# An attention kernel whose opening is written in another order, with the shifts of its first pairs set anew

## The chip, the core and the metric

The kernel runs on one core of a Trainium2 chip. Five engines work beside each other and meet only at semaphores: TensorE (PE, with its weight loads as PEld), VectorE (DVE), ScalarE (ACT), GpSimd (POOL) and SyncE (SP), which here only issues DMAs; ACT issues a few as well. The metric is the device time of one execution in microseconds (us); lower is better.

## The reference

Attention with a causal mask and a bias made of running sums, then two MLPs over all tokens, all in fp32:

```python
def _attn_ref(q, k, v, s):                      # (4, 8, 576, 64), s (4, 8, 576)
    scores = scale * np.matmul(q, k.transpose(0, 1, 3, 2))
    cum = np.cumsum(np.maximum(s, 0.0), axis=-1)
    bias = -(cum[:, :, :, None] - cum[:, :, None, :])
    scores = np.where(causal, -1000000000.0, scores + np.minimum(bias, 0.0))
    scores = scores - np.max(scores, axis=-1, keepdims=True)
    attn = np.exp(scores)
    attn = attn / (np.sum(attn, axis=-1, keepdims=True) + 1e-09)
    return np.matmul(attn, v)

def _moe_ref(x, w_in, w_out, alpha):            # 2304 tokens, 512 -> 2048 -> 512
    h = x @ w_in
    return (np.maximum(h, 0.0) + alpha * np.minimum(h, 0.0)) @ w_out
# the second MLP has r * r, r = max(h, 0), in the middle
```

## The kernel before

Two heads form a pair; there are 16 pairs, numbered 0 to 15. For accuracy each fp32 operand is split into a rounded part (`hi`) and a rest (`lo`), and the matmuls run on the parts. For one pair the work is: load q and k (`load_qk`, a main piece of 256 KB and a tail of 32 KB each), split them (`hi` is one pass, `lo` a subtraction; tiles `hl_q`, `hl_k`), turn them on TensorE (`pp`, L348, and `pp_tail`, L373, into the banks `ps_tr`), copy the turned parts out of the banks into `QS`, `QM`, `KS`, `KH`, and then for five row blocks i and two heads h: scores (`qk`, L419 with `KS`,`QS` and L420 with `KH`,`QM`; L425 for the last block), the row minimum on DVE (`red`, L446), the exponential on ACT (`exp`, L459), the transposes of the result (`tr`, L527), and the two products with v (`pv_a` L561, `pv_b` L577). Rows 64 and 65 of `KH` hold the two parts of the running sum of the pair's heads and meet two rows of ones in `QM`; so L420 of a pair needs those rows. For pair 0 they come straight from the tile `cum_hl` (named pt), for every later pair by a DMA from the DRAM tensor `cumD` (`cum_rows`, L397, two rows of 2304 bytes for each head).

Three things set the order. The opening, L691 to L771, is written out by hand: clearing, loads, splits, transposes and copies of pair 0, the splits of pair 1, and the loads of v for both. After it a list, `PIPE`, gives each step of a pair a place in a period and an offset in periods; a table `RAMP` adds to that place a shift for one step of one pair, and the steps are sorted by the sum. A table `WARM` puts matmuls on zeros, called fillers here (`keep_warm`, L700, out `ps_xa`, in `iv`), behind steps of pair 0. `in_order()` ties the instructions of each engine, and the DMA issues of SP, into that order. Pairs 4 and up go by `PIPE` and the few entries of `RAMP` that the change leaves alone. The MLPs follow, from about 195 us on.

Buffers that matter below: q and k of pairs n and n + 2 share `raw_q0`/`raw_k0` or `raw_q1`/`raw_k1` (so `raw_q0` is pair 0, then 2, then 4), scores have three banks, turned parts four.

Of the kernel before, what the change touches and what calls it, by code (L numbers as in the profile page):

```python
# [8 lines left out]
F32 = mybir.dt.float32  # L9
# [10 lines left out]
def attention_then_two_mlps(  # L20
# [13 lines left out]
    nc = tc.nc  # L34
# [654 lines left out]
        chain["at"] = len(traced)  # L689

    zero = apool.tile([P, S], F32, name="iv", tag="iv", bufs=1)  # L691
    nc.vector.memset(zero, 0.0)
    zero = zero.bitcast(F32R)
    blank = [None]

    def keep_warm(k, cols=512):
        if blank[0] is None:
            blank[0] = ps_x.tile([P, 512], F32, name="ps_xa", tag="ps_x")
        for _ in range(k):
            nc.tensor.matmul(blank[0][:, :cols], zero[:, 0:P], zero[:, :cols], start=True, stop=True)  # L700

    nc.scalar.dma_start(s_sb, s.rearrange("b h c -> (b h) c"))
    load_qk(0, 0)
    load_qk(0, 1, nc.scalar)
    warm = apool.tile([1, 1], F32, name="warm", bufs=1)
    nc.vector.memset(warm, 0.0)
    nc.scalar.activation(warm, warm, AF.Exp)
    keep_warm(10)
    init_persistent(0)
    nc.vector.memset(cum, 0.0)  # L710
    nc.vector.tensor_scalar(s_sb, s_sb, 0.0, None, ALU.max)
    nc.vector.tensor_tensor_scan(cum, s_sb, cum, 0.0, ALU.add, ALU.add)
    for x in range(2):
        load_qk(1, x)

    def kview(a, c):
        return a.rearrange(c, t=4)

    def bank_of(x, h):
        return kview(banks["pp", x, h].bitcast(F32), "p (t c) -> p c t")  # L720

    def qs_out(n, h):
        nc.scalar.activation(kview(QS[n][:, h, P:], "p (c t) -> p c t"), bank_of(0, h), AF.Copy, scale=SCALE)

    def qm_out(h):
        nc.vector.tensor_scalar(kview(QM[0][0:64, h, P:], "p (c t) -> p c t"), bank_of(0, h)[0:64], SCALE, None, ALU.mult)

    def kh_out(n, h, part):
        if part == 1:
            nc.scalar.copy(kview(KH[0][0:64, h, 0 : 4 * P], "p (c t) -> p c t"), bank_of(1, h)[64:128])  # L730
# [5 lines left out]
    hi(0, 0, 0, H1)
    hi(0, 1, 2, H0)
    lo(0, 1, 2, H0)
    hi(0, 1, 2, H1)
# [12 lines left out]
    nc.sync.dma_start(cumD, cum_hl.bitcast(F32))
    load_v(0)
    kh_out(0, 0, 0)
    qm_out(0)
    kh_out(0, 0, 1)
    kh_out(0, 1, 2)
    qs_out(0, 1)
    kh_out(0, 1, 1)
    qm_out(1)  # L760
    pp_tail(0)
    keep_warm(2)
# [814 lines left out]
```

## Time and profile before

| | us |
|---|---|
| median of 3 runs (lowest 950.13, highest 954.41) | 950.86 |
| the profiled execution, as timed | 952.03 |
| its span on the chip | 950.2 |
| PE busy | 936.9 (99%) |
| DVE busy | 770.4 (81%) |
| ACT busy | 607.1 (64%) |
| POOL busy | 280.3 (29%) |

The span runs from the first to the last recorded instruction; 1.83 us of the timed execution lie around it. Matmuls are pipelined and their ends are modelled, so two that follow each other overlap in the records; the distance of two starts tells what one costs. An idle time is given with the engine that ended it, found from the last semaphore that came; where that engine had long been done, it was another, often a DMA.

### The profile page before, as it was taken

The page shows a single profiled execution, that of the slowest core. Times are in us where ns is not written, and L with a number is a line of the kernel's source. Part 1 is how long each engine was busy: PE and PEld are TensorE (multiplying, and loading weights), DVE is VectorE, ACT ScalarE, POOL GpSimd, SP SyncE. Part 2 cuts the span into 40 slices and gives each one's busy share as a digit, 9 for nine tenths or more (in the row PEclk, how much of TensorE's full clock was granted, in tenths as well). Part 3 has the DMA queues.
Part 4 walks back from the last instruction along what each step waited for, and adds up shares of the span by engine and source line. Part 5 has one row for each costly group of instructions (what it writes and reads, how often), then busy time and mean ns, then how long its engine had stood idle before and what let it go on. Part 6 is the DMA issues. An engine that isn't in the chain of part 4 may idle for free.

```text
span 950.2 us, 16991 instructions
## 1 busy us (share of the span) xinstructions
PE 936.9 (99%) x5909; PEld 882.6 (93%) x5909; DVE 770.4 (81%) x1446; ACT 607.1 (64%) x1272; POOL 280.3 (29%) x278
## 2 busy tenths in 40 slices
PE   7999999999999999999999999999999999999998
PEld 6888888899999899999999999999999999999998
DVE  7788878868778987789778878788988888888685
ACT  6999988856566565577666656566445664456432
POOL 7466555134233212322102100344003530045200
PEclk9999999999999999999999999999999999999999
DMA  5787765337666758989568562586755867448384
GB/s 148 197 210 205 198 156 139 87 103 252 208 198 228 275 192 301 341 276 311 168 214 261 184 200 82 163 314 217 244 182 164 273 222 261 146 118 287 118 259 134
DMA packets 141063, 195.69 MB, mean 206 GB/s; under 512 B 50962, under 2 KB 102674, under 8 KB 135602
## 3 DMA queue, kind: packets, MB, share of 16 engines
q1 hardware_dynamic: 140384, 194.11, 65.1%
q8 instruction: 47, 0.77, 0.3%
q10 hardware_dynamic: 594, 0.50, 0.2%
q14 instruction: 38, 0.31, 0.1%
HBM read 140.47 MB, written 45.83 MB: 196 GB/s over the span
## 4 chain that ended last, share of the span: by engine, by line
PE 91%; DVE 3%; DMA 2%; ACT 1%; SPq 1%; issue 1%; POOL 0%; ACTq 0%; DVEq 0%; POOLq 0%
PE acc L1253 18%; PE po L935 18%; PE ph L637 12%; PE ph L1440 6%; PE a L1094 5%; PE b L1094 5%; PE c L1094 5%; PE ps_tr L527 5%; PE ps_xb L577 3%; PE d L1094 3%; PE ps_xa L561 2%; PE ps_sc L419 2%; PE ps_sc L420 2%; PE ps_tr L348 2%; PE ps_sc L425 2%; DMA raw_w<-in_moe_w_in_dram 1%
## 5 line engine op out<-in xcount | busy, mean ns | idle before, releaser
L1253 PE MATMUL acc<-th,w2s 128*128 128x384 f32 x1008 | 177.6, 335 | 0.0
L1253 PEld LDWEIGHTS acc<-th,w2s 128*128 128x128 f32 x1008 | 175.2, 188 | 0.0
L935 PE MATMUL po<-gs,wo_hi 128*128 128x512 f32 (+1 forms) x768 | 166.3, 336 | 0.7 <-DVE gs L1418 0.5
L935 PEld LDWEIGHTS po<-gs,wo_hi 128*128 128x128 f32 x768 | 122.8, 188 | 14.3 <-DVE gs L1418 1.1
L637 PE MATMUL ph<-xs,wi_hi 128*128 128x384 f32 x512 | 130.6, 335 | 2.1 <-DVE gg L664 1.9
L985 ACT CAST th<-g 128x768 fp32r<-128x768 f32 x84 | 70.2, 836 | 78.5 <-PE acc L1253 57.0
L986 DVE TENSOR_TENSOR th<-g,th 128x768 fp32r<-128x768 f32 x84 | 80.2, 955 | 24.8 <-ACT th L985 24.6
L935 PE MATMUL po<-gs,wo_lo 128*128 128x256 f32 (+1 forms) x384 | 99.1, 337 | 0.0
L637 PEld LDWEIGHTS ph<-xs,wi_hi 128*128 128x128 f32 x512 | 90.6, 188 | 4.0 <-DVE gg L664 2.7
L986 DVE TENSOR_TENSOR w1h<-w1f,w1h 128x512 fp32r<-128x512 f32 x96 | 74.3, 777 | 22.2 <-ACT w1h L985 22.0
L142 POOL TENSOR_TENSOR wc<-cv_t,wc 128x512 uint32<-128x512 uint32 x24 | 37.0, 1549 | 165.3 <-DVE cv_t L138 121.1
L637 PE MATMUL ph<-xs,wi_lo 128*128 128x384 f32 x256 | 85.6, 334 | 0.0
L985 ACT CAST w1h<-w1f 128x512 fp32r<-128x512 f32 x96 | 53.8, 565 | 39.6 <-PE b L1094 25.4
L446 DVE CUSTOM_DVE_ANT_0 pr<-ps_sc,mask 128x128 f32<-128x128 f32 (+3 forms) x128 | 61.8, 486 | 14.3 <-PE ps_sc L420 11.3
L142 POOL TENSOR_TENSOR wf<-cv_t,wf 128x512 uint32<-128x512 uint32 x32 | 45.2, 1413 | 94.3 <-DVE cv_t L138 71.0
L1105 POOL TENSOR_TENSOR g<-g 128x384 f32<-128x384 f32 x24 | 23.8, 990 | 162.2 <-ACT g L1104 162.1
L459 ACT ACTIVATE pr<-pr,nmax 128x128 f32<-128x128 f32 (+3 forms) x128 | 71.2, 557 | 0.4
L935 PEld LDWEIGHTS po<-gs,wo_lo 128*128 128x128 f32 x384 | 59.2, 188 | 7.9
L1094 PE MATMUL a<-xc,w1h 128*128 128x384 f32 x288 | 58.5, 335 | 0.0
L1440 PE MATMUL ph<-xc,wi_hi 128*128 128x384 f32 x224 | 57.6, 337 | 0.6 <-DVE xc L986 0.6
L1094 PE MATMUL c<-xc,w1h 128*128 128x384 f32 x288 | 58.0, 334 | 0.0
L1094 PE MATMUL b<-xc,w1h 128*128 128x384 f32 x288 | 57.8, 335 | 0.0
(204 smaller groups left out, 2130.2 us busy)
## 6 DMA issues: line engine op xcount, KB each, us to landing
w2s<-w2D SPq DMA_DIRECT2D x42, 1024.0 KB
w1f<-w1D SPq DMA_DIRECT2D x72, 256.0 KB
raw_w<-in_moe_w_in_dram SPq DMA_DIRECT2D x32, 512.0 KB
w2D<-whl SPq DMA_DIRECT2D x16, 896.0 KB
raw_w<-in_moe_w_out_dram SPq DMA_DIRECT2D x24, 512.0 KB
wo_lo<-loD SPq DMA_DIRECT2D x29, 256.0 KB
iv<-sD SPq DMA_DIRECT2D x32, 144.0 KB
raw_q<-in_q_dram SPq DMA_DIRECT2D x16, 256.0 KB
```

Of the source, the lines that this page charges most:

```text
L142: nc.gpsimd.tensor_tensor(d, tt, d, ALU.add)
L446: nc.vector.tensor_tensor_reduce(o, banks.pop(("s", i, h))[:, :w], m, -1.0, first, ALU.add, ALU.min, nmax[:, h : h + 1])
L459: nc.scalar.activation(o, o, AF.Exp, bias=m, scale=-1.0, accum_out=sums_of[n][:, i, h : h + 1])
L527: last = nc.tensor.transpose(ps[:, z * P : (z + 1) * P], pr[:, c0 : c0 + P], ident)
L577: last = nc.tensor.matmul(xb[64 * h : 64 * h + 64, c0 : P + TAIL], vv[:, j, h, :], pt[:, h, j, c0:], start=(j == 0), stop=(j == 4),)
L637: nc.tensor.matmul(ph[h][:, :HT], ws[a][:, kb * P : (kb + 1) * P], xs[kb][:, bb, h * HT : (h + 1) * HT], start=(cnt == 0), stop=(cnt == 3 ...
L935: nc.tensor.matmul(acc, ws[a][:, m * P : (m + 1) * P], gs[:, bb, c_], start=first_ and z == 0, stop=lst and z == 2, skip_group_check=True,)
L985: a = nc.scalar.copy(dst[:, 0], src)
L986: v = nc.vector.tensor_sub(dst[:, 1], src, dst[:, 0].bitcast(F32))
L1094: nc.tensor.matmul(pt[:, :HT], hl[:, a, c0 + kb * P : c0 + (kb + 1) * P], xc[i][:, b, kb, :], start=(first and cnt == 0), stop=(cnt == 5), ...
L1253: nc.tensor.matmul(acc[m][:, :HT], ws[:, y, (2 * q + qq) % 4, m * P : (m + 1) * P], th[:, x, qq, :], start=(fresh and q == 0 and qq == 0 a ...
L1440: nc.tensor.matmul(acc[:, :HT], hl[a][:, c0 + kb * P : c0 + (kb + 1) * P], xp[i][:, b, kb, :], start=(fresh and cnt == 0), stop=(cnt == 5) ...
```

## The change

Only the opening and the two tables change. The memsets of pair 0 that DVE did (`init_persistent(0)`: rows of ones in `QM`, the heads of `QM` and `QS`) go to POOL, one by one between other work; the scan starts from the zeros of `iv` and not from a cleared tile. The main pieces of q and k of pair 0 are both issued by SP, their tails by ACT. The splits of pair 0 are shared out in quarters among ACT, DVE and POOL, with k ahead of q. v of pair 0 is loaded ahead of the sums' rows, and the store to `cumD` goes from SP to ACT. The copies out of the banks change engine in part. Of pair 1, k is loaded and split ahead of q. `RAMP` has 290 entries for 130; 227 steps move, 78 of pair 0, 73 of pair 1, 54 of pair 2 and 22 of pair 3. `WARM` has 17 fillers for 15, and the opening 12 for 16.

```diff
@@ opening, before
-    nc.scalar.dma_start(s_sb, s.rearrange("b h c -> (b h) c"))
-    load_qk(0, 0)
-    load_qk(0, 1, nc.scalar)
...
-    nc.scalar.activation(warm, warm, AF.Exp)
-    keep_warm(10)
-    init_persistent(0)
-    nc.vector.memset(cum, 0.0)
-    nc.vector.tensor_scalar(s_sb, s_sb, 0.0, None, ALU.max)
-    nc.vector.tensor_tensor_scan(cum, s_sb, cum, 0.0, ALU.add, ALU.add)
-    for x in range(2):
-        load_qk(1, x)
...
-    for h in range(2):
-        for x in range(2):
-            pp(0, x, h)
-            keep_warm(1)
-    qs_out(0, 0)
-    for h in range(2):
-        nc.sync.dma_start(KH[0].bitcast(F32)[64:66, h, :], cum_hl.bitcast(F32)[h : h + 1])
-    nc.sync.dma_start(cumD, cum_hl.bitcast(F32))
-    load_v(0)
...
-    for x in range(2):
-        hi(1, x, 2)
-    for x in range(2):
-        lo(1, x, 2)
-    init_persistent(1)
-    load_alpha()
-    load_v(1)
@@ opening, after
+    def load_main(n, x, e):
+        b, hp = pairs[n]
+        e.dma_start(
+            raw_qk[x][n % 2][:, 0:8, :].rearrange("p (h t) d -> p h (t d)", h=2),
+            (q, k)[x][b, 2 * hp : 2 * hp + 2][:, 0 : 4 * P].rearrange("h (p t) d -> p h (t d)", t=4),
+        )
...
+    nc.vector.memset(zero, 0.0)
+    nc.gpsimd.memset(ptl[0][0:64, :, 4, :], 0.0)
+    load_main(0, 0, nc.sync)
+    nc.scalar.dma_start(s_sb, s.rearrange("b h c -> (b h) c"))
+    load_main(0, 1, nc.sync)
+    nc.vector.memset(warm, 0.0)
+    nc.gpsimd.memset(QM[0].bitcast(F32)[:, :, 0:TAIL], 0.0)
+    keep_warm(8)
+    nc.gpsimd.memset(raw_v[0][0:64, 4, :, :], 0.0)
+    nc.vector.tensor_scalar(s_sb, s_sb, 0.0, None, ALU.max)
+    load_tail(0, 0, nc.scalar)
+    nc.vector.tensor_tensor_scan(cum, s_sb, zeros, 0.0, ALU.add, ALU.add)
+    load_qk(1, 1, nc.sync)
+    load_tail(0, 1, nc.scalar)
+    nc.gpsimd.memset(QS[0].bitcast(F32)[:, :, 0:TAIL], 0.0)
+    hi(0, 1, 2, H0)
+    hi(0, 0, 0, H0)
+    load_qk(1, 0, nc.sync)
+    hi(0, 1, 0, H1)
+    nc.scalar.copy(cum_hl[:, 0, :], cum)
+    hi(0, 1, 0, HT_)
+    keep_warm(1)
+    lo(0, 1, 1, H0)
+    nc.gpsimd.memset(QM[0].bitcast(F32)[64:66, :, TAIL:], 1.0)
+    load_v(0)
+    lo(0, 0, 1, H0)
+    pp(0, 1, 0)
+    nc.gpsimd.memset(rs_[0], 0.0)
+    hi(0, 0, 0, slice(4, 9))
+    lo(0, 1, 2, H1)
+    lo(0, 0, 2, HT_)
+    nc.scalar.activation(warm, warm, AF.Exp)
+    pp(0, 0, 0)
+    pp(0, 1, 1)
+    nc.vector.tensor_sub(cum_hl[:, 1, :], cum, cum_hl[:, 0, :].bitcast(F32))
+    ks_out(0, 0)
+    nc.sync.dma_start(KH[0].bitcast(F32)[64:66, 0, :], cum_hl.bitcast(F32)[0 : 1])
+    hi(1, 1, 2)
+    hi(1, 0, 2)
+    keep_warm(2)
+    nc.scalar.dma_start(cumD, cum_hl.bitcast(F32))
+    kh_out(0, 0)
+    lo(0, 1, 1, HT_)
+    pp_tail(0)
+    lo(0, 0, 1, H1)
+    ks_out(1, 1)
+    pp(0, 0, 1)
+    keep_warm(1)
+    kh_out(1, 0)
+    nc.sync.dma_start(KH[0].bitcast(F32)[64:66, 1, :], cum_hl.bitcast(F32)[1 : 2])
+    lo(1, 1, 2)
+    load_alpha()
+    qs_out(0, 1, 0)
+    qs_out(0, 0, 1)
+    qm_out(1, 0)
+    lo(1, 0, 2)
+    qm_out(0, 1)
+    q_tail(0)
+    init_persistent(1)
+    load_v(1)
+    k_tail(0)
@@ tables
-    WARM = {("qk_11", 0): 1, ("qk_20", 0): 2, ("qk_21", 0): 3, ("qk_30", 0): 3, ("qk_31", 0): 2, ("qk_40", 0): 2, ("tr_0", 0): 1, ("tr_1", 0): 1}
+    WARM = {('qk_20', 0): 4, ('qk_21', 0): 2, ('qk_30', 0): 2, ('tr_0', 0): 2, ('tr_1', 0): 4, ('qk_01', 0): 1, ('qk_00', 0): 1, ('pp_q0', 1): 1}
```

What stands in a row on SP, from the last piece of the first loads to the coefficients `alpha`; before:

```order
L292 DMA raw_k1_133<-in_k_dram 128x1x64
L751 DMA KH0_122<-pt_142 2x1x576 x2
L752 DMA cumD_118<-pt_142 64x1x576
L298 DMA raw_v0_125<-in_v_dram 128x4x64 x2
L301 DMA raw_v0_125<-in_v_dram 64x2x64
L70 DMA alpha_sb_82<-in_moe_alpha_dram 128x16x1
```

and after:

```order
L292 DMA raw_q1_132<-in_q_dram 128x1x64
L298 DMA raw_v0_125<-in_v_dram 128x4x64 x2
L301 DMA raw_v0_125<-in_v_dram 64x2x64
L774 DMA KH0_122<-pt_142 2x1x576
L787 DMA KH0_122<-pt_142 2x1x576
L70 DMA alpha_sb_82<-in_moe_alpha_dram 128x16x1
```

The store to `cumD` has left SP, and v of pair 0 (`raw_v0`) stands ahead of the rows for `KH0`. Further on in the same queue, from the tail of k of pair 2; before:

```order
L292 DMA raw_k0_124<-in_k_dram 128x1x64
L288 DMA raw_k1_133<-in_k_dram 128x2x256
L292 DMA raw_k1_133<-in_k_dram 128x1x64
L397 DMA KH1_131<-cumD_118 2x2x576
L105 DMA raw_w_354<-in_moe_w_in_dram 128x4x256
L288 DMA raw_q1_132<-in_q_dram 128x2x256
```

and after:

```order
L292 DMA raw_k0_124<-in_k_dram 128x1x64
L288 DMA raw_k1_133<-in_k_dram 128x2x256
L292 DMA raw_k1_133<-in_k_dram 128x1x64
L105 DMA raw_w_376<-in_moe_w_in_dram 128x4x256
L397 DMA KH1_131<-cumD_118 2x2x576
L288 DMA raw_q1_132<-in_q_dram 128x2x256
```

The first load of MLP weights (`raw_w`) now stands ahead of the rows of sums for pair 1 (`KH1`). On PE, around the first scores of pair 1 (`KS1`, `KH1`), with the last steps of pair 0 (`pr` is the exponential of a row block); before:

```order
L527 MATMUL ps_tr_390<-ident_75,pr_331 128x128 x2
L527 MATMUL ps_tr_390<-ident_75,pr_344 128x128 x2
L425 MATMUL ps_sc_396<-KS0_121,QS0_119 128x288
L425 MATMUL ps_sc_396<-KS0_121,QS0_119 64x288
L425 MATMUL ps_sc_396<-KH0_122,QM0_120 64x288
L425 MATMUL ps_sc_396<-KH0_122,QM0_120 128x288
L527 MATMUL ps_tr_408<-ident_75,pr_331 128x128
L527 MATMUL ps_tr_408<-ident_75,pr_344 128x128
L527 MATMUL ps_tr_415<-ident_75,pr_372 128x128 x4
L419 MATMUL ps_sc_420<-KS1_130,QS1_128 128x128
L420 MATMUL ps_sc_420<-KH1_131,QM1_129 128x128
```

and after:

```order
L425 MATMUL ps_sc_389<-KS0_121,QS0_119 128x288
L425 MATMUL ps_sc_389<-KS0_121,QS0_119 64x288
L425 MATMUL ps_sc_389<-KH0_122,QM0_120 64x288
L425 MATMUL ps_sc_389<-KH0_122,QM0_120 128x288
L419 MATMUL ps_sc_404<-KS1_130,QS1_128 128x128
L420 MATMUL ps_sc_404<-KH1_131,QM1_129 128x128
L527 MATMUL ps_tr_407<-ident_75,pr_314 128x128
L527 MATMUL ps_tr_407<-ident_75,pr_323 128x128
L419 MATMUL ps_sc_417<-KS1_130,QS1_128 128x128
L420 MATMUL ps_sc_417<-KH1_131,QM1_129 128x128
L527 MATMUL ps_tr_421<-ident_75,pr_314 128x128 x2
L527 MATMUL ps_tr_421<-ident_75,pr_323 128x128 x2
```

Of the transposes L527 of pair 0, 16 stood ahead of the first L420 of pair 1 (the ten shown and six earlier); now six do, and ten stand behind it.

## Rows read from the trace of the kernel before

**Rows 1.** Page, part 1: busy time, share of the span, instructions by engine.

```profile
PE 936.9 (99%) x5909; PEld 882.6 (93%) x5909; DVE 770.4 (81%) x1446; ACT 607.1 (64%) x1272; POOL 280.3 (29%) x278
```

**Rows 2.** Windows: length, busy time by engine, PEclk, DMA share, GB/s.

```profile
6.10:11.00 4.90, 3.38 (x25) 2.76 (x26) 3.61 (x7) 3.08 (x6) 4.20 (x6) 1.00 0.21 63
11.00:17.00 6.00, 4.76 (x37) 4.06 (x35) 3.49 (x13) 4.00 (x13) 4.88 (x9) 1.00 0.77 131
17.00:23.50 6.50, 5.57 (x39) 4.93 (x39) 5.86 (x19) 5.00 (x14) 4.24 (x5) 1.00 0.71 209
23.50:45.00 21.50, 21.50 (x187) 18.60 (x189) 16.87 (x58) 19.93 (x63) 8.18 (x8) 1.00 0.71 194
45.00:185.00 140.00, 140.00 (x1232) 121.51 (x1229) 114.81 (x377) 125.69 (x401) 72.64 (x76) 1.00 0.66 173
```

**Rows 3.** Timeline of PE: start, length, line, operands, count; pair 1 begins.

```profile
22.39 0.82 PE L527 MATMUL ps_tr<-ident,pr 128*128 128x128 f32 x6
22.96 0.30 PE L419 MATMUL ps_sc<-KS,QS 128*128 128x128 f32 x1
23.47 0.30 PE L420 MATMUL ps_sc<-KH,QM 66*128 66x128 f32 x1 [0.20 <-POOL hl_k L338]
```

**Rows 4.** Timeline of SP (SPq), its DMA issues: start, length.

```profile
4.78 0.53 SPq L292 DMA_DIRECT2D raw_k<-in_k_dram  x1
...
8.36 1.26 SPq L751 DMA_DIRECT2D KH<-pt  x2
9.67 0.66 SPq L752 DMA_DIRECT2D cumD<-pt  x1
10.37 1.18 SPq L298 DMA_DIRECT2D raw_v<-in_v_dram  x2
...
12.35 0.59 SPq L70 DMA_DIRECT2D alpha_sb<-in_moe_alpha_dram  x1
...
19.27 1.07 SPq L397 DMA_DIRECT2D KH<-cumD  x1
20.39 0.39 SPq L105 DMA_DIRECT2D raw_w<-in_moe_w_in_dram  x1
```

**Rows 5.** Timeline of POOL: splits of pairs 0 and 1, a memset, L71.

```profile
4.80 0.41 POOL L333 TENSOR_SCALAR hl_k<-raw_k 128x256 fp32r<-128x256 f32 x1 [1.01 <-DMA raw_k<-in_k_dram]
5.30 2.02 POOL L338 TENSOR_TENSOR hl_k<-raw_k,hl_k 128x256 fp32r<-128x256 f32 x1
7.94 0.72 POOL L333 TENSOR_SCALAR hl_k<-raw_k 128x320 fp32r<-128x320 f32 x1 [0.62 <-DMA raw_k<-in_k_dram]
8.74 0.86 POOL L338 TENSOR_TENSOR hl_k<-raw_k,hl_k 128x320 fp32r<-128x320 f32 x1
...
12.24 1.41 POOL L338 TENSOR_TENSOR hl_k<-raw_k,hl_k 128x576 fp32r<-128x576 f32 x1
13.70 1.06 POOL L271 MEMSET QM<- 2x1152 f32 x1
...
15.80 0.20 POOL L71 TENSOR_SCALAR beta_sb<-alpha_sb 128x16 f32<-128x16 f32 x1
```

**Rows 6.** Timeline of DVE: relu and scan of s, one copy out of a bank.

```profile
4.41 0.39 DVE L711 TENSOR_SCALAR prl<-prl 32x576 f32<-32x576 f32 x1
4.83 1.58 DVE L712 TENSOR_TENSOR_SCAN prl<-prl 32x576 f32<-32x576 f32 x1
...
8.27 0.67 DVE L726 TENSOR_SCALAR QM<-ps_tr 64x512 fp32r<-64x512 f32 x1
```

**Rows 7.** Timeline of PE: the first L420 of all.

```profile
11.04 0.28 PE L420 MATMUL ps_sc<-KH,QM 66*128 66x128 f32 x1
```

**Rows 8.** Timeline of PE: first two and last two of the ten fillers.

```profile
2.22 1.22 PE L700 MATMUL ps_xa<-iv 128*128 128x512 f32 x2 [2.22 <-DVE warm L706]
...
5.46 0.63 PE L700 MATMUL ps_xa<-iv 128*128 128x512 f32 x2
```

**Rows 9.** Window right behind the issue of raw_w; columns as in Rows 2.

```profile
21.30:23.60 2.30, 2.10 (x19) 1.99 (x18) 2.27 (x8) 2.27 (x6) 2.22 (x3) 1.00 0.91 257
```

More of the change, by code (lines that the diff above doesn't have):

```diff
@@ L691, in attention_then_two_mlps @@
     zero = apool.tile([P, S], F32, name="iv", tag="iv", bufs=1)
-    nc.vector.memset(zero, 0.0)
-    zero = zero.bitcast(F32R)
-    blank = [None]
+    zeros, blank = zero[0:BH], [None]
+    warm = apool.tile([1, 1], F32, name="warm", bufs=1)
     def keep_warm(k, cols=512):
@@ L698, in keep_warm, with load_tail @@
             blank[0] = ps_x.tile([P, 512], F32, name="ps_xa", tag="ps_x")
+        z = zero.bitcast(F32R)
         for _ in range(k):
-            nc.tensor.matmul(blank[0][:, :cols], zero[:, 0:P], zero[:, :cols], start=True, stop=True)
-    nc.scalar.dma_start(s_sb, s.rearrange("b h c -> (b h) c"))
-    load_qk(0, 0)
-    load_qk(0, 1, nc.scalar)
-    warm = apool.tile([1, 1], F32, name="warm", bufs=1)
-    nc.vector.memset(warm, 0.0)
-    nc.scalar.activation(warm, warm, AF.Exp)
-    keep_warm(10)
-    init_persistent(0)
-    nc.vector.memset(cum, 0.0)
-    nc.vector.tensor_scalar(s_sb, s_sb, 0.0, None, ALU.max)
-    nc.vector.tensor_tensor_scan(cum, s_sb, cum, 0.0, ALU.add, ALU.add)
-    for x in range(2):
-        load_qk(1, x)
+            nc.tensor.matmul(blank[0][:, :cols], z[:, 0:P], z[:, :cols], start=True, stop=True)
+    def load_main(n, x, e):
[4 more added lines that the diff above has]
+        )
+    def load_tail(n, x, e):
+        b, hp = pairs[n]
+        e.dma_start(raw_qk[x][n % 2][:, 8, :], (q, k)[x][b, 2 * hp : 2 * hp + 2][:, 4 * P : S])
     def kview(a, c):
@@ L720, in bank_of @@
         return kview(banks["pp", x, h].bitcast(F32), "p (t c) -> p c t")
[L722 to L730, printed above, removed]
-        else:
-            evac(kview(KS[n][:, h, 0 : 4 * P], "p (c t) -> p c t"), bank_of(1, h), part // 2)
@@ L734, in attention_then_two_mlps @@
-    H0, H1 = slice(0, 4), slice(4, 9)
-    hi(0, 0, 0, H0)
[L736 to L739, printed above, removed]
-    lo(0, 1, 2, H1)
-    nc.scalar.copy(cum_hl[:, 0, :], cum)
-    lo(0, 0, 1, H0)
-    lo(0, 0, 1, H1)
-    nc.vector.tensor_sub(cum_hl[:, 1, :], cum, cum_hl[:, 0, :].bitcast(F32))
-    for h in range(2):
-        for x in range(2):
-            pp(0, x, h)
-            keep_warm(1)
-    qs_out(0, 0)
-    for h in range(2):
-        nc.sync.dma_start(KH[0].bitcast(F32)[64:66, h, :], cum_hl.bitcast(F32)[h : h + 1])
@@ L752, in attention_then_two_mlps, with scaled, qs_out @@
-    nc.sync.dma_start(cumD, cum_hl.bitcast(F32))
-    load_v(0)
[L754 to L762, printed above, removed]
+    def scaled(dst, src, e):
+        if e == 0:
+            nc.scalar.activation(dst, src, AF.Copy, scale=SCALE)
+        else:
+            nc.vector.tensor_scalar(dst, src, SCALE, None, ALU.mult)
+    def qs_out(n, h, e):
+        scaled(kview(QS[n][:, h, P:], "p (c t) -> p c t"), bank_of(0, h), e)
@@ new lines, in qm_out, with ks_out, kh_out @@
+    def qm_out(h, e):
+        scaled(kview(QM[0][0:64, h, P:], "p (c t) -> p c t"), bank_of(0, h)[0:64], e)
+    def ks_out(h, e):
+        evac(kview(KS[0][:, h, 0 : 4 * P], "p (c t) -> p c t"), bank_of(1, h), e)
+    def kh_out(h, e):
+        evac(kview(KH[0][0:64, h, 0 : 4 * P], "p (c t) -> p c t"), bank_of(1, h)[64:128], e)
+    H0, H1, HT_ = slice(0, 4), slice(4, 8), slice(8, 9)
+    nc.vector.memset(zero, 0.0)
+    nc.gpsimd.memset(ptl[0][0:64, :, 4, :], 0.0)
+    load_main(0, 0, nc.sync)
```

2 lines of the change are left out of this document (1 added, 1 removed).

## The prediction

> **What bounds the kernel now.** I read the page's busy times first: PE is busy for 99% of the span, DVE for 81%, ACT for 64% [rows 1]. So time can only be won where PE is idle or works on zeros. The windows say where that is [rows 2]: from 23.5 to 185 us PE is busy in every microsecond (21.50 of 21.50, 140.00 of 140.00), while it lacks 1.52 us between 6.1 and 11, 1.24 between 11 and 17 and 0.93 between 17 and 23.5, and these stretches hold fillers besides. A change in the opening is worth what it does to the moment from which PE is never without work again.
>
> That moment is 23.47: L419 of pair 1 starts at 22.96, and L420 behind it only at 23.47 [rows 3]. The row names POOL, but what L420 needs of POOL is the memset of the ones in `QM` of pair 1, done at 13.70 + 1.06 = 14.76 [rows 5]. Its other need is the rows of sums in `KH`, a DMA that SP issued from 19.27 to 20.34 [rows 4]; so they landed 3.13 us after their issue ended. SP had been issuing without a pause since 8.36, when the low part of the sums was ready: 20.34 - 8.36 = 11.98 us of issues in a row [rows 4]. The opening thus ends when SP has worked through its queue, and the question is how early that queue now gets to the rows of pair 1.
>
> **The change, part by part.** *SP's queue.* From the first rows of `KH` for pair 0 to the end of the rows for pair 1 the 11.98 us change by three moves. The loads of v of pair 0 go ahead: 12.35 - 10.37 = 1.98 less. The store to `cumD` goes to ACT: 10.37 - 9.67 = 0.70 less. The load of `raw_w` comes in: 0.39 and a gap of 0.04, 0.43 more [rows 4]. That leaves 9.73. Where does this stretch begin? SP issues six pieces before it, as now, and those end at 4.78 + 0.53 = 5.31; with v behind them SP is free at 5.31 + 1.98 = 7.3 [rows 4]. The rows of pair 0 also wait until the tail of k of pair 0 has landed, which in the trace was at the latest 7.94, when POOL took it up [rows 5]. So 7.3 to 7.9; I take the middle, 7.6, since the tail is now issued earlier but on a queue that the trace does not show in this use. The issue for pair 1 then ends at 7.6 + 9.73 = 17.33 (17.0 to 17.7), and with the 3.13 us of rows 3 and 4 its data land at 20.46 (20.2 to 20.8), which is 3.0 us before 23.47.
>
> *Work that changes sides.* Ten transposes L527 that stood ahead of this L420 now stand behind it. Six of them took 22.96 - 22.39 = 0.57 [rows 3], so ten are 0.95 us that PE still has to do after the moment when it had done them before. Nothing else crosses: all fillers stand ahead in both kernels, and all scores of pair 0 too. **The sum: 3.01 - 0.95 = 2.06 us earlier.** From there on PE has its rows without a pause, as before, and carries the lead to the end.
>
> *Does PE get there in time?* The first L420 of pair 0, at 11.04 [rows 7], comes behind this chain now: POOL takes up the main piece of k at 4.80 as before (it is second in its queue in both kernels), 0.41, then the memset that DVE did, which on POOL took 1.06, and a small one of 0.2: 6.5. Its subtraction of 256 columns costs 0.69 at the rate of the 320 columns at 8.74 (0.86), or 2.02 as at 5.30 [rows 5]: 7.2 to 8.5. Four transposes of half a microsecond and three copies of 0.67 on DVE [rows 6] follow: 9.7 to 11.0, 0 to 1.3 us earlier than now. What DVE is spared (it reaches s only at 4.41 and ends the scan at 6.41 [rows 6]) lies beside this chain. From the first L420 on PE has at most 4.76 + 5.57 = 10.33 us of work up to 23.5 [rows 2], less the 0.95, plus 0.3 for two more fillers (half of a pair that took 0.63 [rows 8]): 9.7. It reaches pair 1 at 19.4 to 20.7 if nothing else holds it, and the records overlap, so less rather than more. That is just ahead of the rows of sums; I take these as what ends last.
>
> The 2.02 us at 5.30 fell together with the scan on DVE (4.83 to 6.41) and the subtractions behind it, while the 0.86 at 8.74 ran beside a copy out of PSUM [rows 5, 6]. The Trainium skill (SBUF — State Buffer, section Who interferes with whom) says that a DVE instruction with two SBUF inputs blocks a GpSimd instruction that reads SBUF, but not one that only writes. That speaks against this change, which has POOL subtract while DVE subtracts: by it the 11.0 holds and PE comes at 20.7; by the shorter row at 19.4. The trace agrees with the rule here, and in the sum both ends lie at or before 20.8.
>
> *The rest of the opening.* For pair 1 POOL needs, behind its last work for pair 0, all of the 13.65 - 9.60 = 4.05 us of passes but one subtraction of 1.41 until k is split [rows 5]: 2.64 and 0.2 on top of 7.2 to 8.5, so 10.0 to 11.3 against 13.65. q is split behind L71, a new wait: L71 ran at 15.80 without waiting [rows 5] and now stands ahead of the subtraction of q, of the six memsets for pair 1 and of the splits of pair 2. `alpha` is issued at 7.6 + 1.30, takes 0.59 [rows 4], and by 3.13 us like the rows above lands at 12.6; q is then ready at 12.6 + 0.2 + 1.41 = 14.2, about when PE turned it before, behind k (13.65 and later). So q of pair 1 gains nothing, k gains 2.3 us or more, and the copies of k are out of the way when q comes. The issue of `cumD` on ACT, 0.66 [rows 4], waits for the low part of the sums and holds the copies into `KH` behind it; those wait for DVE's copy of the same bank anyway, and without that cover it is 0.66 us on the first scores, within their 1.3.
>
> *Pairs 1 to 3 in the table.* 149 steps of these pairs move, the work is the same. PE never waits there now [rows 2], so nothing can be won, and any wait that arises is a loss; ACT, with 19.93 of 21.50 busy, is the nearest one to cause it [rows 2]. I take zero, and up to 1 us of loss for the range.
>
> **Rivals.** *The weights' load is in the way.* The 512 KB of `raw_w` now go ahead of the rows of sums. Right behind its issue the engines moved 257 GB/s at a share of 0.91 [rows 9]; at that rate 512 KB are 2.0 us. If the rows wait for all of it, they land at 22.5 and the lead is 0.1: 950.8. For it: that stretch was full. Against it: the issue of the rows takes 1.07 us itself [rows 4], during which half of the load is through, and the same rows had the loads of pair 3 ahead of them before and kept to 3.13. The Trainium skill (DMA: Bandwidth & Descriptors, section Queues, rings and completion order) says that each DMA engine consumes the descriptors of a queue in ring order, which is this rival; no run here shows how much of `raw_w` sits on the engines of those two rows.
>
> *The rows of sums come early.* The first such rows, for pair 0, were issued by 8.36 + 0.6 and had landed when L420 ran at 11.04 without a wait [rows 4, 7], so within 2.1 us. With that the rows of pair 1 land at 19.4, PE itself is last at 19.4 to 20.0, and with L419's 0.1 less than now the lead is 23.1 - 19.7 - 0.95 = 2.4 to, at an arrival of 19.0, 3.1 us. I price it at 2.9: 948.0. Against it: those rows came from SBUF, the later ones from DRAM in a fuller queue.
>
> *PE falls back to its slow clock: slower.* The first two fillers took 1.22 us, the last two 0.63 [rows 8], the two levels of 1.2 and 2.4 GHz, while the column of the granted clock shows 1.00 in every window [rows 2]. Between its fillers at the start and the first scores PE is busy for 3.38 of 4.90 us now, with six fillers [rows 2]; after the change three fillers and the same eighteen transposes stand in about four, with a gap of one to two microseconds before the second half of k. If it fell back there, the 9.7 us behind the first L420 would double. It decides once PE loses more than 23.47 - 0.95 - 20.0 = 2.5 us by it; with half of the stretch at the lower level it loses 4.85, the lead becomes -2.3, and the time 953.2. Against it: the gaps of today, about as long, do no harm.
>
> **How the numbers follow.** The sum is made against the profiled execution: its span 950.2 becomes 948.1, its time 952.03, with 1.83 around the span, 949.9. The median of the runs is 950.86; less 2.1 it is 948.8. Chances: the forecast 0.57, the weights' load in the way (lead 0 to 1) 0.20, rows early (lead 2.6 to 4) 0.13, slow clock 0.10. A measurement of this kernel can tell about 0.5%, 4.8 us, from no change. A lead of that size is not to be had, since idle and fillers ahead of 23.47 are needed in part by the splits: 0.03 for faster, mostly the spread of the runs (950.13 to 954.41). Slower by that much needs the clock low for most of the stretch: 0.04. Within: 0.93. For the range I take a lead of 3.9 at one end (rows early) and a loss of 0.5 at the other, which holds the weights' load at its full price and a microsecond lost in pairs 1 to 3: 946.9 to 951.4.
>
> **What would show it.** In the profile after: SP's issue of the rows for pair 1 ends at 17.0 to 17.7; the first L420 of pair 1 starts at 20.2 to 20.8 with an idle time before it; PE's windows are full from there on; POOL's subtraction of the second half of k lasts nearer to 2 than to 0.7 us. The forecast is wrong if L420 starts with nothing waited for (PE was last, or the rows came early), if the issue ends as said and L420 starts at 22 or later (the load), or if idle time appears in pairs 1 to 3.

## The result, and the profile after

The changed kernel is slower: a median of 959.62 us over 6 runs (956.48 to 963.50) against 951.12 over 6 runs of the kernel before (950.10 to 954.41), a ratio of 1.0087 with a 95% interval from 1.0068 to 1.0105. The forecast was 948.8, with a range of 946.9 to 951.4. The profiled execution took 958.51 us, its span is 956.1 (950.2 before).

The windows of the changed kernel, cut as in [rows 2] (length, busy time of PE, PEld, DVE, ACT and POOL, granted clock, DMA share, GB/s):

```profile
6.10:11.00 4.90, 3.15 (x20) 2.39 (x20) 2.58 (x6) 2.09 (x6) 2.88 (x6) 1.00 0.45 104
11.00:17.00 6.00, 5.82 (x30) 5.60 (x30) 4.27 (x16) 4.29 (x14) 5.00 (x9) 0.54 0.75 148
17.00:23.50 6.50, 6.47 (x47) 5.82 (x45) 4.18 (x16) 5.07 (x15) 5.22 (x7) 0.90 0.64 190
23.50:45.00 21.50, 20.76 (x176) 17.88 (x176) 16.80 (x59) 19.36 (x62) 7.58 (x8) 1.00 0.66 172
45.00:185.00 140.00, 137.06 (x1201) 118.74 (x1202) 113.30 (x364) 122.15 (x387) 71.50 (x74) 1.00 0.65 170
```

Two things are new. The clock column shows 0.54 where it showed 1.00: PE was granted half of its clock, 1.2 of 2.4 GHz, from 11.5 to 18.3 us. And the two long windows are no longer full: PE idles for 0.74 us in one and 2.94 in the other. The timeline of PE names the three places, one in the opening and two in the attention (start, length, line, operands, count, idle before and what ended it); the second row answers to the last of [rows 3]:

```profile
10.19 0.28 PE L373 MATMUL ps_tr<-ident_r,hl_q 128*128 128x128 f32 x1 [1.32 <-POOL hl_q L338]
...
22.78 0.28 PE L420 MATMUL ps_sc<-KH,QM 66*128 66x128 f32 x1
...
46.77 0.53 PE L348 MATMUL ps_tr<-ident_r,hl_k 128*128 128x128 f32 x4 [2.51 <-POOL hl_k L338]
...
85.15 0.30 PE L420 MATMUL ps_sc<-KH,QM 66*128 66x128 f32 x1 [1.17 <-DMA sD<-rT]
```

Pair 1 starts 0.69 us earlier than before (22.78 for 23.47), which the ten transposes moved behind it (0.95) more than use up. Then PE waits 2.51 us for k of pair 4 and 1.17 us for a DMA that L420 of pair 6 needs (the row names a store to `sD`, the second profile below a copy into `KH`). What holds k of pair 4 stands on POOL:

```profile
28.42 1.41 POOL L338 TENSOR_TENSOR hl_q<-raw_q,hl_q 128x576 fp32r<-128x576 f32 x1
42.98 1.02 POOL L505 TENSOR_TENSOR x<-x,iv 128x384 f32<-128x384 f32 x1 [13.15 <-DMA iv<-sD]
43.95 0.60 POOL L507 TENSOR_TENSOR xT<-xT,iv 128x192 f32<-128x192 f32 x1
44.51 0.68 POOL L333 TENSOR_SCALAR hl_k<-raw_k 128x576 fp32r<-128x576 f32 x1
45.27 1.45 POOL L338 TENSOR_TENSOR hl_k<-raw_k,hl_k 128x576 fp32r<-128x576 f32 x1
```

POOL stands still for 13.15 us in front of L505, the scaling of the output of pair 0 (step `nrm`), which waits for `iv`, the inverse row sums that come back through DRAM (`ds` stores them, `di` loads them, L497). The split of k of pair 4 stands behind it; that it could have run long before is shown by the next run. In the table `nrm` of pair 0 has moved by -0.79, `di` by -0.42. The Trainium skill (PSUM — Partial Sum Buffer, section Engine vs sequencer instructions) calls the queues of ScalarE, VectorE and GpSimdE strictly first in, first out; these five rows agree.

### The profile page after: what moved, and what is told of

Same layout as the page of the kernel before. It is cut to its first block, busy times and chain, and to the rows that moved or that the text cites. A ratio compares the mean times of both kernels' runs of the same rounds, so it can differ in the third digit from the quotient of the medians.

```text
span 956.1 us, 16981 instructions
## 1 busy us (share of the span) xinstructions
PE 941.2 (98%) x5907; PEld 886.9 (93%) x5907; DVE 771.2 (81%) x1444; ACT 608.0 (64%) x1274; POOL 281.5 (29%) x280
## 4 chain that ended last, share of the span: by engine, by line
PE 87%; DMA 4%; ACT 4%; DVE 3%; issue 1%; POOL 0%; ACTq 0%; SPq 0%; DVEq 0%
PE acc L1280 18%; PE po L962 17%; PE ph L637 11%; PE ph L1467 6%; PE a L1121 5%; PE b L1121 5%; PE c L1121 5%; PE ps_tr L527 4%; PE d L1121 3%; PE ps_xb L577 2%; PE ps_sc L419 2%; DMA raw_w<-in_moe_w_in_dram 2%; PE ps_xa L561 2%; PE ps_sc L420 2%; PE ps_tr L348 2%; PE ps_sc L425 2%
## 5 line engine op out<-in xcount | busy, mean ns | idle before, releaser
L637 PE MATMUL ph<-xs,wi_hi 128*128 128x384 f32 x512 | 130.9, 336 | 1.9 <-DVE gg L664 1.9
L637 PEld LDWEIGHTS ph<-xs,wi_hi 128*128 128x128 f32 x512 | 91.0, 189 | 3.5 <-DVE gg L664 2.3
L637 PE MATMUL ph<-xs,wi_lo 128*128 128x384 f32 x256 | 85.9, 336 | 0.0
L459 ACT ACTIVATE pr<-pr,nmax 128x512 f32<-128x512 f32 (+3 forms) x128 | 71.1, 556 | 0.6 <-DVE nmax L446 0.4
```

The costliest lines, as they stand in the source:

```text
L459: nc.scalar.activation(o, o, AF.Exp, bias=m, scale=-1.0, accum_out=sums_of[n][:, i, h : h + 1])
L637: nc.tensor.matmul(ph[h][:, :HT], ws[a][:, kb * P : (kb + 1) * P], xs[kb][:, bb, h * HT : (h + 1) * HT], start=(cnt == 0), stop=(cnt == 3 ...
```

## The experiments

**Taking the shift out.** The changed kernel with `nrm` of pair 0 back in its place:

```diff
-RAMP = {... ('nrm', 0): -0.79, ...}
+RAMP = {...}
```

> The changed kernel with the shift -0.79 of nrm of pair 0 taken out of the table, so that on POOL the two products L505 and L507 of pair 0 stand behind the split of k of pair 4 again. Theory (POOL holds k of pair 4 back behind a wait for iv): the idle of 2.51 us in front of L348 at 46.77 goes, k of pair 4 is split by 36 to 40 us, and the time falls by 2.5 us to about 957. Rival (k of pair 4 or its banks are late anyway): an idle of 1 us or more stays in front of L348 and the time falls by less than 1 us. The fall of the clock in the opening stays in both.

Measured: 952.71 us (12 runs), a ratio to before of 1.0009 (0.9994 to 1.0024): 6.9 us of the 8.5 are gone. On POOL the split is done long before, and L505 waits for nobody:

```profile
30.05 1.43 POOL L338 TENSOR_TENSOR hl_k<-raw_k,hl_k 128x576 fp32r<-128x576 f32 x1
45.10 1.28 POOL L142 TENSOR_TENSOR wf<-cv_t,wf 128x512 uint32<-128x512 uint32 x1 [13.62 <-DVE cv_t L138]
46.34 0.68 POOL L333 TENSOR_SCALAR hl_q<-raw_q 128x576 fp32r<-128x576 f32 x1
46.98 1.02 POOL L505 TENSOR_TENSOR x<-x,iv 128x384 f32<-128x384 f32 x1
```

The split ends at 31.48, no idle time stands in front of L348, and the mechanism held; the price of 2.51 us was far too small. So the next runs ask whether this wait is the whole cause, and why it costs more than its idle time.

**Putting the shift into the kernel before.**

```diff
-RAMP = {("qk_10", 0): ...
+RAMP = {("nrm", 0): -0.79, ("di", 0): -0.42, ("qk_10", 0): ...
```

> The kernel before with two of the new shifts alone, nrm -0.79 and di -0.42 of pair 0, so that POOL's L505 and L507 of pair 0, which wait for iv, stand ahead of the split of k of pair 4. Theory (this wait on POOL is what makes the changed kernel slower): PE idles for 2 us or more in front of L348 of pair 4 at about 43 to 46 us, and the time rises by 2.5 to 7 us to 953.6 to 958. Rival (the loss needs the new opening or the other shifts as well): PE idles for less than 0.5 us there and the time stays within 1 us of 951.1.

Measured: 959.60 us, 1.0085 (1.0072 to 1.0098). Two numbers of the table, in the old opening, cost as much as the whole change, and more than the 953.6 to 958 expected. One row of PE and four windows of this kernel (columns as above) show what the wait draws after it:

```profile
46.46 0.75 PE L348 MATMUL ps_tr<-ident_r,hl_k 128*128 128x128 f32 x4 [3.41 <-POOL hl_k L338]
```

```profile
44.00:46.00 2.00, 0.00 (x0) 0.00 (x0) 1.11 (x2) 0.06 (x1) 1.92 (x2) 0.74 0.74 222
46.00:48.00 2.00, 1.54 (x8) 1.51 (x9) 0.00 (x0) 0.15 (x1) 2.00 (x3) 0.50 0.20 31
48.00:50.00 2.00, 2.00 (x14) 1.56 (x14) 1.16 (x3) 2.00 (x7) 1.92 (x3) 0.50 0.73 249
50.00:52.00 2.00, 2.00 (x17) 1.52 (x14) 0.00 (x0) 0.19 (x2) 1.82 (x2) 0.55 0.01 5
```

PE idles for 3.41 us, and then works at 0.50 of its clock until nearly 52 us, some 5.3 us: about 2.7 us more, so 6 for one wait. The start of one matmul, before and in this run, bears it out:

```profile
57.78 0.28 PE L420 MATMUL ps_sc<-KH,QM 66*128 66x128 f32 x1
```

```profile
63.69 0.28 PE L420 MATMUL ps_sc<-KH,QM 66*128 66x128 f32 x1
```

PE is 5.91 us late there, after being 0.09 us early at 41 us. Of this 4.38 are left at 323 us, where PE waits 1.05 us for DVE in front of L637 and not 1.95 as in the kernel before. The opening of this run also shows 0.50 from 14.3 to 17.7 us, where the kernel before shows 1.00, and that cost nothing by 41 us.

**The changed kernel once more**, unaltered, for a second profile:

> The changed kernel once more, for a second profile. Its first showed idle times of 2.51 us in front of L348 of pair 4 and 1.17 us in front of L420 of pair 6, but taking nrm out of its place won 6.9 us at the median. Theory (the landing of iv varies, and with it the stall): the idle in front of L348 is 2.5 to 6 us here, and differs from 2.51. Rival (the rest lies elsewhere): it is 2.5 us again and other idle times have grown.

Measured: 957.11 us in its one run, an idle time of 2.00 us in front of L348 and 0.97 in front of L420 of pair 6; both smaller, so neither expectation fits. But here the clock fell behind the wait (0.57 from 46 to 50 us), which it had not in the first profile, where it fell at 329 to 332 us. That later fall does not belong to the wait: e2_nrm and e7_before_sp, which have no such wait, show one at 324 to 327 us. The wait has a price of its own in each execution.

**Covering the wait with matmuls.**

```diff
+        if (op, n) == ("pp_k0", 4):
+            spare = ps_x.tile([P, 512], F32, name="ps_xa", tag="ps_x")
+            for _ in range(20):
+                nc.tensor.matmul(spare[:, :256], KS[0][:, 0, 0:P], KS[0][:, 0, 0:256], start=True, stop=True)
+            in_order()
         emit(op, n)
```

> The changed kernel with twenty 256-column matmuls whose result nobody reads in front of L348 of pair 4, where PE idles for 2 to 2.5 us: they cover the idle at 0.12 us each and change nothing else of weight. Theory (part of the price is the granted clock, which fell to 0.50 some microseconds behind that idle in two of three profiles that have it): the clock stays at 1.00 between 44 and 60 us, PE is as late as before, and the time falls by 1.5 to 3.5 us, to 956 to 958. Rival (the price is the wait alone): the time stays within 0.7 us of 959.6, and the clock falls somewhere else.

Measured: 960.40 us, 1.0077 (1.0055 to 1.0099). The time is within 0.8 us of 959.6, a little more than the rival allowed, and the clock did not stay at 1.00: it stood at 0.50 from 49.6 to 53.0 us. But the run does not separate the two prices, because in the profiled execution (961.66 us) the wait had grown past its cover. SP's issues, POOL and PE:

```profile
35.14 3.96 SPq L298 DMA_DIRECT2D raw_v<-in_v_dram  x2
39.19 1.80 SPq L301 DMA_DIRECT2D raw_v<-in_v_dram  x1
41.05 1.23 SPq L497 DMA_DIRECT2D iv<-sD  x2
```

```profile
45.09 1.02 POOL L505 TENSOR_TENSOR x<-x,iv 128x384 f32<-128x384 f32 x1 [15.21 <-DMA iv<-sD]
```

```profile
44.27 2.54 PE L927 MATMUL ps_xa<-KS 128*128 128x256 f32 x20
49.27 0.60 PE L348 MATMUL ps_tr<-ident_r,hl_k 128*128 128x128 f32 x4 [2.46 <-POOL hl_k L338]
```

The issue of two loads of v took 3.96 us; in the first profile of the changed kernel the same two took 1.24. So `iv` left 2.9 us later (41.05 for 38.16), and PE was held for 5.0 us (44.27 to 49.27). The loads ahead of these two were the same in both (k, weights and q, 1.1 MB), so why their issue took 2.7 us longer is not shown. A wait that differs so much between executions may well be the spread of this kernel's runs (956 to 963); that too is not shown. (In this build one store, `w0D`, also stands five issues earlier on SP, behind the wait.)

**Two edits on that backlog.** First `iv` ahead of v of pair 2, then also 512 KB of weights behind both:

```diff
-('di', 0): -0.42        # first
+('di', 0): -0.52
-('lw', 3): 0.44         # second, with the first
+('lw', 3): 0.72
```

> The changed kernel with nrm left where the change put it, on POOL ahead of the split of k of pair 4, but with di of pair 0 at -0.52 for -0.42: SP issues the two loads of iv ahead of the loads of v of pair 2, which took 1.24 and 1.80 us in front of them. Theory (POOL's order only hurts because iv lands late): iv is issued about 3 us earlier, at 35 us, L505 starts near 40, k of pair 4 is split by 43.7, the idle in front of L348 falls below 0.5 us and the time falls by 4 to 7 us, to 953 to 955.6. Rival (SP then waits itself until the sums of pair 0 have been stored to sD, and iv is no earlier): the idle stays at 2 us or more and the time within 1 us of 959.6.

> The kernel with iv loaded ahead of v of pair 2 (955.65 us: iv issued by 35.95, POOL's L505 started at 41.77, idle of 1.59 us in front of L348), and besides that the 512 KB of raw_w that SP issued at 33.0 put behind v of pair 2 (lw of pair 3 at 0.72 for 0.44). Theory (iv waits in the queue behind the bytes issued ahead of it): at the 200 to 260 GB/s of this stretch 512 KB are 2.0 to 2.6 us, so L505 starts at 39.2 to 39.8, k of pair 4 is split by 43.6, the idle in front of L348 is under 0.3 us and the time falls by 2 to 3.5 us, to 952.2 to 953.7. Rival (iv is slow by itself, a load that is read 64 times over from DRAM): L505 stays near 41.8, the idle at 1.5 us and the time within 0.7 us of 955.65.

Measured: 955.65 us, 1.0037 (1.0023 to 1.0051), for the first; 953.37 us, 1.0016 (0.9999 to 1.0034), for both. The first gave the time that its theory had at the edge, but an idle time between the two expectations: issued 3.5 us earlier, `iv` was used only 1.2 us earlier (41.77 for 42.98), and PE idled for 1.59. SP and POOL of the first, then of the second:

```profile
34.65 1.30 SPq L497 DMA_DIRECT2D iv<-sD  x2
```

```profile
41.77 1.00 POOL L505 TENSOR_TENSOR x<-x,iv 128x384 f32<-128x384 f32 x1 [11.91 <-DMA iv<-sD]
```

```profile
35.01 1.40 SPq L497 DMA_DIRECT2D iv<-sD  x2
```

```profile
40.10 1.01 POOL L505 TENSOR_TENSOR x<-x,iv 128x384 f32<-128x384 f32 x1 [9.88 <-DMA iv<-sD]
...
42.39 1.42 POOL L338 TENSOR_TENSOR hl_k<-raw_k,hl_k 128x576 fp32r<-128x576 f32 x1
```

With 512 KB less ahead of it `iv` is there 1.7 us sooner, the split ends at 43.81, and no idle time stands in front of L348 any more, though POOL's order is the changed one. (This profile is of one of its slower executions, 956.27 us; the rest of its delay lies elsewhere, at pair 6 and in a fall of the clock at 327 us.) So the order alone does not cost; it costs because `iv` comes late, and 512 KB ahead of it in SP's queue are 1.7 us of that. In the changed kernel some 1.4 MB are issued in front of it (288 KB each of k, q and v and 512 KB of weights, from 32.3 us on). The Trainium skill (DMA: Bandwidth & Descriptors, section Queues, rings and completion order) says that each DMA engine takes descriptors in ring order; the two runs agree with it.

**What one wait costs.** Two matmuls L420, which start at 41.30 and 57.78 in the kernel before, show it in every profile (us; the last column is how much more than 16.48 lies between them):

| | idle in front of L348 | clock at 0.50 in or behind it | first | second | lost |
|---|---|---|---|---|---|
| before | none | no | 41.30 | 57.78 | 0 |
| e2_nrm | none | no | 40.73 | 57.62 | 0.41 |
| e12_di_lw | none | no | 41.98 | 58.86 | 0.40 |
| e10_di | 1.59 | no | 41.12 | 59.81 | 2.21 |
| e1_fill, below | 1.69 | no | 40.45 | 59.24 | 2.31 |
| changed kernel | 2.51 | no | 41.47 | 61.08 | 3.13 |
| the same again | 2.00 | 46.3 to 49.7 | 41.58 | 62.19 | 4.13 |
| e8_before_nrm | 3.41 | 45.0 to 51.8 | 41.21 | 63.69 | 6.00 |
| e11_stall_fill | 2.46 behind the cover | 49.6 to 53.0 | 41.63 | 65.12 | 7.01 |

The new order loses 0.4 us here without any wait (e8_before_nrm has the old one). Beyond that, a wait costs about its own length where the clock holds, and 1.6 to 2.6 us more where it falls (in e11_stall_fill the whole wait is 5.0 us, cover included).

**The clock in the opening.** Six more fillers into the gap of 1.32 us; the same with `nrm` in its place; and the kernel before without six of its fillers:

```diff
-    keep_warm(2)          # changed kernel, ahead of pp_tail(0)
+    keep_warm(8)
-            keep_warm(1)  # kernel before, behind each pp(0, x, h)
-    keep_warm(2)          # kernel before, behind pp_tail(0)
```

> The changed kernel with six more 512-column fillers (8 for 2) in front of the tail transposes of pair 0, where PE idled for 1.32 us from 8.87 on, ahead of the fall of the granted clock to 0.50 from 11.5 to 18.2. Theory (the gap brings the clock down): the clock shows 1.00 in every window up to 30 us and PE is 3.4 us ahead at 18 us; then the rows of sums decide, at the latest 18.58 + 3.13 = 21.7, so the first L420 of pair 1 starts between 19.4 and 21.7 (22.78 now) and the time falls by 1.1 to 3.4 us, to 956 to 958.5 against 959.6. Rival (the clock falls for another reason, such as the lighter load of PE up to 8 us): 0.50 still stands from about 11.5 on, and the time stays within 0.5 us of 959.6.

> Both edits together: the six more fillers and nrm of pair 0 back in its place. If the two losses are separate they add up: 3.6 to 5.9 us, a time of 953.7 to 956. What then stays against the kernel before is the idle of 1.17 us at 85 us and the second fall of the clock near 329 us (1.7 us). If one feeds the other, the sum is smaller than that of the two runs apart by over 1 us.

> The kernel before without the six fillers in its opening (one behind each group of four transposes, two behind the tails). Theory (gaps of PE bring the clock down): idle times of PE between 8 and 13 us grow from 0.84 and 0.91 to over 1.2 us and the granted clock falls to 0.50 for some microseconds in the opening, the time rises by 2 to 4 us to 953 to 955. Rival (those fillers only fill, and the clock has another cause): clock 1.00 throughout, time within 0.5 us of 951.1.

Measured: 958.97 us (6 runs), 1.0081 (1.0058 to 1.0105); 952.62, 1.0013 (0.9998 to 1.0027); and 953.32, 1.0016 (1.0003 to 1.0028). The gap does bring the clock down: all six profiles of the changed opening without the fill show 0.50 there (from 9.8 to 12.5 us on), and the three with it show 1.00 up to the first scores of pair 1; bared, the kernel before idles 1.40 us from 8.19 on and runs at 0.50 from 10 to nearly 20 us:

```profile
9.59 0.70 PE L348 MATMUL ps_tr<-ident_r,hl_k 128*128 128x128 f32 x4 [1.40 <-POOL hl_k L338]
```

Its median is some 2 us higher; in its profile PE is 0.5 us late from 30 us on. But in the changed kernel the fill won next to nothing, 0.65 us and 0.1, both within the intervals, which neither expectation of e1_fill had. SP and PE of the filled kernel (e1_fill) say why; the profile is of its fastest execution, 953.15 us, and the other five took 957.90 to 961.39:

```profile
16.77 0.91 SPq L105 DMA_DIRECT2D raw_w<-in_moe_w_in_dram  x1
17.72 0.41 SPq L397 DMA_DIRECT2D KH<-cumD  x1
```

```profile
20.30 0.25 PE L419 MATMUL ps_sc<-KS,QS 128*128 128x128 f32 x1
22.04 0.30 PE L420 MATMUL ps_sc<-KH,QM 66*128 66x128 f32 x1 [1.49 <-DMA KH<-cumD]
```

PE is there 2.3 us sooner (L419 at 20.30 for 22.64) and waits for the rows of sums, which land 3.91 us behind the end of their issue, not 3.13. The slow clock had been hidden behind that wait. In e3_fill_nrm the wait is 1.78 us, and the clock falls behind it, to 0.50 from 22.5 to 26.0 us: PE comes to pair 1 ahead of the kernel before and is 1.0 us behind it at 41 us. (This run's 952.62 lies below its 953.7 to 956, because `nrm` alone gave more than it was priced at.)

**The rows of sums ahead of the weights**, on top of filler and `nrm`:

```diff
-('dk', 1): 0.15
+('dk', 1): 0.0
```

> The kernel with fillers and nrm in its place (952.6 us, where the first L420 of pair 1 waited 1.78 us and started at 22.30, 3.87 us after the issue of its rows of sums had ended), with the rows of sums for pair 1 issued ahead of the load of raw_w again. Theory (the weights' load delays the rows, by its issue and by its data): the issue ends at about 17.3, the rows land 3.1 us later as in the kernel before, L420 starts at 20.4 to 20.7 with hardly a wait, and the time falls by 1.6 us to about 951. Rival (the rows take 3.9 us behind any queue): L420 starts at 21.2 and the time falls by about 1 us. If the time does not fall although L420 comes earlier, the lead is lost again in pairs 1 to 6, and the trace shows where.

Measured: 952.54 us (12 runs), 1.0009 (0.9996 to 1.0022). SP and PE, first of e3_fill_nrm and then of this run:

```profile
18.02 0.41 SPq L397 DMA_DIRECT2D KH<-cumD  x1
```

```profile
22.30 0.30 PE L420 MATMUL ps_sc<-KH,QM 66*128 66x128 f32 x1 [1.78 <-DMA KH<-cumD]
```

```profile
17.20 0.98 SPq L397 DMA_DIRECT2D KH<-cumD  x1
18.23 0.38 SPq L105 DMA_DIRECT2D raw_w<-in_moe_w_in_dram  x1
```

```profile
21.17 0.30 PE L420 MATMUL ps_sc<-KH,QM 66*128 66x128 f32 x1 [0.45 <-DMA KH<-cumD]
```

The rows land 2.99 us behind their issue again, where it had been 3.87: 0.9 us is what the 512 KB cost ahead of them. L420 starts 1.13 us sooner than in e3_fill_nrm, but at 21.17 and not by 20.7, since the issue ended at 18.18 and not at 17.3. Pair 1 now starts 2.30 us earlier than before, 1.35 after the ten transposes. Yet the median is no better than that of the kernel before. In the profile PE keeps a lead of 1.2 us up to 279 us and loses half of it at 280.42, in a wait for DVE that the kernel before does not have. The rows of L637 behind the next long wait, shown below it for the kernel before and for this one, are only 0.59 us apart, and the spans are 950.2 and 949.5.

```profile
280.42 0.62 PE L962 MATMUL po<-gs,wo_hi 128*128 128x512 f32 x2 [0.38 <-DVE gs L668]
```

```profile
322.98 0.61 PE L637 MATMUL ph<-xs,wi_hi 128*128 128x384 f32 x2 [1.95 <-DVE gg L664]
```

```profile
322.39 0.62 PE L637 MATMUL ph<-xs,wi_hi 128*128 128x384 f32 x2 [1.86 <-DVE gg L664]
```

**SP's share alone**, in the kernel before:

```diff
+    load_v(0)
     for h in range(2):
         nc.sync.dma_start(KH[0].bitcast(F32)[64:66, h, :], ...)
-    nc.sync.dma_start(cumD, cum_hl.bitcast(F32))
-    load_v(0)
+    nc.scalar.dma_start(cumD, cum_hl.bitcast(F32))
```

> The kernel before with the change in SP's queue alone: v of pair 0 loaded ahead of the rows of sums of pair 0, the store to cumD issued by ACT. The prediction's step (the opening ends when SP has worked through its queue): the issue of the rows of pair 1 ends 2.7 us earlier, at about 17.7, and L420 of pair 1 and all behind it come earlier by up to that, time 949 to 950. Rival (PE, DVE and ACT were as late as SP, since PE had waited for the rows only 0.20 us): the issue ends early, L420 of pair 1 moves by 0.2 us at most, and the time stays within 0.5 us of 951.1.

Measured: 952.33 us, 1.0000 (0.9991 to 1.0010). SP and PE:

```profile
16.96 1.47 SPq L397 DMA_DIRECT2D KH<-cumD  x1
```

```profile
23.17 0.28 PE L420 MATMUL ps_sc<-KH,QM 66*128 66x128 f32 x1
```

The issue of the rows of pair 1 ended at 18.43, 1.9 us earlier, and L420 of pair 1 started at 23.17, without a wait, 0.30 us earlier. The rival was right but for a tenth of a microsecond: SP was the last of several that were about equally late.

## Why the prediction was wrong, point by point

- **Behind the opening, with the term for pairs 1 to 3 in the table: the step that failed.** The prediction let PE have its rows without a pause from pair 1 on and carry the lead to the end. It priced the table at zero, with up to 1 us of loss, because PE never waits there, and named ACT, busy for 19.93 of 21.50 us, as the nearest to cause a wait. That says nothing on a step that moves ahead of another on an in-order engine. The wait came from POOL, busy for 8.18 of 21.50 us [rows 2]. It came by two shifts of pair 0, `nrm` and `di`, which run as late as 43 us and which the term did not count, and it held back k of pair 4. These shifts are worth 6.9 us when `nrm` is taken out and 8 us when both are put in alone. (The count of 149 steps holds three shifts of zero, so 146 of these pairs move.) The rows to price it were in the trace of the kernel before (SP, POOL, PE):

```profile
35.88 1.41 SPq L301 DMA_DIRECT2D raw_v<-in_v_dram  x1
...
41.68 1.20 SPq L497 DMA_DIRECT2D iv<-sD  x2
```

```profile
47.39 1.01 POOL L505 TENSOR_TENSOR x<-x,iv 128x384 f32<-128x384 f32 x1 [0.44 <-DMA iv<-sD]
```

```profile
42.97 0.46 PE L348 MATMUL ps_tr<-ident_r,hl_k 128*128 128x128 f32 x4
```

  There `iv` was used 4.5 us after the end of its issue (42.88 to 47.39), with POOL waiting for it. In the new order SP issues it behind L301: 37.29 + 1.20 + 4.5 = 43.0. Two products and a split, some 3.7 us, follow on POOL: 46.7, where PE wants k at 42.97. A loss of 3.7 us, before any fall of the clock, and the sign of the forecast would have turned. That 43.0 is what the first profile shows (42.98) is luck: SP got through L301 only at 38.11 and issued `iv` for 1.70 us, and `iv` was then used 3.1 us later, not 4.5. The idle time was 2.51 and not 3.7, since PE too came 1.3 us later to L348.
- **SP's queue: the size was off.** The issue for pair 1 ended at 18.58, not at 17.0 to 17.7. The stretch was 9.62 us long, as worked out (9.73), but began at 8.96: the loads of v, priced at 1.98 from a row at 10.37, took 4.42 us in their new place behind the other loads (2.97 for the first two, 1.45 for the third). The tail of k, the other thing that these rows wait for, was no earlier (8.89, below), for the 7.9 taken.
- **What ends the opening.** That the opening ended when SP had worked through its queue was half the truth. PE had waited for it only 0.20 us [rows 3], and SP's share alone moved it by 0.30.
- **Rival, the weights in the way: right in kind.** It had a chance of 0.20 and up to 2.0 us. The landing took 3.9 us with `raw_w` ahead and 3.0 without, so 0.9. The rival of rows that come early, in 2.1 us, was seen nowhere.
- **Rival, the slow clock: it came, and cost little there.** It had a chance of 0.10 and a lead of -2.3 us. The clock stood at 0.50 for some 6.8 us, but the rows of sums would have ended last at about 22.5 in any case (18.58 + 3.9), and PE came at 22.78.
- **Does PE get there in time?** The first L420 of pair 0 ran at 11.80, outside of 9.7 to 11.0. POOL's subtraction (L338 at 6.88) took 0.73, not 2 us; it ran beside a subtraction of DVE for 0.1 us only, so the reason for the 2 us was hardly put to the test. What was late was the tail of k, which ACT, its new issuer, waited for until 8.89, and behind it the tail of q (the idle of 1.32 us above):

```profile
8.89 0.24 ACT L329 CAST hl_k<-raw_k 128x64 fp32r<-128x64 f32 x1 [2.86 <-DMA raw_k<-in_k_dram]
```

  With the clock held PE still reached L419 of pair 1 at 20.30 (e1_fill), within 19.4 to 20.7.
- **The forecast itself.** With the clock held, the weights behind and `nrm` in its place the lead at pair 1 is 1.35 us for the 2.06 forecast, and it does not show in the median. So the gain was of the right kind and too large, and the loss was missed. The chance of 0.04 for a time slower by 4.8 us or more was given to a slow clock for most of the opening; what came had another cause.

Open: in front of L420 of pair 6 PE waits about 1 us in five of the profiles (1.17 and 0.97 in the changed kernel, 0.81, 1.12 and 1.18 in e1_fill, e3_fill_nrm and e12_di_lw) and hardly or not in the others. No run was made on it. In the first profile it makes PE 1.4 us later (from 3.29 late at 61 us to 4.72 at 85), and the fall of the clock at 329 us 1.1 more; with the wait at pair 4 these are the 5.9 us of that profile. But `nrm` is worth 6.9 us at the median, for 5.3 between the two profiled executions (958.51 and 953.24), and how the 6.9 are made up is not shown. The longer waits of single executions and the fall of the clock behind them can do it, as the table of what one wait costs shows; how often each of them comes is not shown.

## What to carry to other kernels

Before a step moves forward on an in-order engine, write down what it waits for, when that lands, and what stands behind it; a wait in front of work that the busy engine needs costs at least its length, whatever the averages say, and here nearly twice that where the clock fell behind it. A load inherits the backlog of its queue: its landing is priced with the bytes ahead of it in the new order (512 KB were 0.9 us and 1.7 us here), not with its old duration. And an earlier start, or a slower clock, counts only as far as nothing else ends last: look for the second wait before paying for the first.

## What the hardware showed that had not been expected

- Issuing a load is not a fixed cost. The two main loads of v of a pair took 1.18 us on SP in the kernel before [rows 4] and 2.97 behind six other loads, both for pair 0. Those of pair 2 took 3.96 in e11_stall_fill and 1.24 in the first profile of the changed kernel, with the same 1.1 MB issued ahead of them.
- PE's granted clock does not follow an idle time of a given length. It fell behind 1.32 us of idle time in the opening of the changed kernel, in both profiles, and not behind 2.51 us at 46.77 in the first, though it did behind 2.00 us in the second; in front of the same matmul L637, in the first MLP, an idle time of 1.94 us drew a fall in the changed kernel, and one of 1.95 drew none in the kernel before.
